# Regrouped blocks of a pair taken from partition quarters of different halves, the second block's transfers issued by ScalarE

## The chip, the cores and the metric

The kernel runs on one core of one Trainium2 chip. The metric is the device time of one execution in microseconds (us), as the median of several executions. The engines are TensorE (PE in the profile, its weight loads PEld), VectorE (DVE), ScalarE (ACT), GpSimd (POOL) and SyncE (SP). SP only issues DMA transfers here; ACT and POOL issue some as well, between their own instructions. In the profile "ACTq" and "SPq" are the issuing sides of ACT and SP.

## The reference

Two parts follow each other. The first filters a sequence along its length with a real FFT; the second is an MLP with a SoLU activation and a layer norm.

```python
x: (8, 3136, 256)   filt_r, filt_i: (1569, 256)
X = rfft(x, axis=1);  y = irfft(X * (filt_r + 1j * filt_i), n=3136, axis=1)

x = y.reshape(25088, 256)            # 25088 tokens
h = x @ w_in                         # (25088, 1024)
e = exp(h - max(h));  sm = e / (sum(e) + 1e-9)
solu = h * sm
ln = (solu - mean(solu)) / sqrt(var(solu) + 1e-6) * g_ln
out = ln @ w_out                     # (25088, 256), float32
```

## The kernel before

**The spectrum part.** Each of the eight sequences goes through a two-stage DFT written as small matmuls, a product with the filter, and the way back. Its results for two sequences at a time lie in the tile `y`. Sequence 0 and part of sequence 1 are done ahead. Then sequence e + 1 is transformed in pieces beside the MLP of sequence e, at steps that the table `PLAN` gives. A "spectrum stage" below is a stretch of steps in which pieces of `Spectrum.forward`, `multiply` and `inverse` run. For each piece ACT issues two loads into SBUF at the end of an even step: `t2` (line L286, 512 KB, called `t<-d` in the profile) and the DFT table `de` (L677, 256 KB). The last spectrum stage ends near 1250 us; from about 1350 us on only the MLP runs, which is called the plain stage.

**The MLP.** Tokens go in blocks of 128, 196 blocks, and two blocks are a pair, 98 pairs. A step `k` belongs to a block; an even and an odd step make a pair `j`. Both matmuls use Strassen's scheme in Winograd's form over a pair: seven products per pair for `w_in` (`product(j, m)`, m from 1 to 7, L717) and seven for `w_out` (`project(p, m)`, L838), with sums of operands by POOL (`sum_of`, L696). Each takes PE about 0.88 us. I call them product m and projection m.

The order of work is written out by hand in `step(k)`, under a manual schedule; each engine takes its instructions in that order.

- Even step of pair j: product 1; projection 5 of pair j-5; product 2; product 6 and its copy to SBUF by ACT (`keep`, L727); projection 3 of pair j-5 and an output half by ACT (`keep_out`, L850); projection 4; the regrouping of the second block of pair j-3; product 7; then, at the end of the step, the loads of the spectrum pieces.
- Odd step: product 5 and its copy to SBUF by ACT (`keep`); projection 1 of pair j-4 with an output half; projection 2; an exponential by ACT (`exponential`, L749); product 3; product 4; projections 6 and 7; the rest.

Product 5 adds to the PSUM bank of product 6, and product 3 adds to that of product 5, so a copy by ACT stands between each two. VectorE's `finish` steps (L738, L741) complete `h` and its running minimum.

**Turning and regrouping.** For the second matmul the block (tokens by features) has to be transposed. VectorE transposes 32 by 32 squares (`turn`, L781) of four blocks into one tile `turn` of two pairs (a group g). Its four partition quarters then hold 32 feature rows each of mixed tokens. `regroup(p, i)` makes from one quarter of 32 partitions a block `solu_t` of 128 partitions, in four transfers of 128 KB, each from the same 32 partitions to one quarter of the destination. A pair has two such blocks (i = 0 and 1), eight transfers in all, which SP issues (L793). The first block's four are issued early in the even step, after `turn`; the second block's four after projection 4, which is the last to read the buffer that the second block goes into (`solu_t1`, two buffers). `a` is the quarter that is read. `out_half` picks the matching column of the scales `rss`, and `store_out` the matching rows of the output; both follow from `a`. `deviations` (L804) and `regroup_deviations` (L810) send the scales through DRAM, also by SP.

Of the kernel before, what the change touches and what calls it, by code (L numbers as in the profile page):

```python
# [17 lines left out]
P = 128  # L18
# [76 lines left out]
def kernel(  # L95
# [10 lines left out]
    nc = tc.nc  # L106
# [290 lines left out]
    with ExitStack() as st:  # L397
# [50 lines left out]
        second = Spectrum(1, None, None, None)  # L448
# [103 lines left out]
        for n in range(16):  # L552
            (nc.sync, nc.scalar)[n % 2].dma_start(
                out=t2_0[NH * (n % 4):NH * (n % 4) + NH, n // 4, :], in_=rows_x[n:n + 1])
# [29 lines left out]
        for i0, n, rows in ((0, 4, P), (4, 4, P), (8, NP - 9, P), (NP - 1, 1, NQ)):  # L584
            f, at = filters[i0]
            nc.sync.dma_start(
                out=f_dram[i0:i0 + n].rearrange("i u q k c -> (u q) i (k c)")[0:rows],
                in_=f[0:rows, at:at + n].rearrange("p i k c -> p i (k c)"))
# [85 lines left out]
    def load_de(sp, u):  # L674
# [6 lines left out]
    turns, variances, solu_ts, solu_sums, rs_rows, rss, pos, ots = (  # L681
        {} for _ in range(8))
# [101 lines left out]
    def regroup(p, i):  # L784


        g, second = divmod(p, 2)
        turned = turns[g].rearrange("p (k q) b i -> p k q (b i)", q=4)
        a = 2 * second + i
        st = upool.tile([P, KF, P], FP32, name=f"solu_t_{p}_{i}", tag=f"solu_t{i}")  # L790
        solu_ts[p, i] = st[:, 0:KF // 2, :], st[:, KF // 2:KF, :]
        for q in range(4):
            nc.sync.dma_start(out=st[32 * q:32 * q + 32, :, :],  # L793
                              in_=turned[32 * a:32 * a + 32, :, q, :])

    def deviations(p):
        g, second = divmod(p, 2)
# [45 lines left out]
    def out_half(p, i, n):  # L843
        if p not in ots:
            ots[p] = wk2.tile([P, 2, C], FP32, name=f"ot_{p}", tag="ot")
        return ots[p][:, i, P * n:P * n + P], rss[p // 2][:, 2 * (p % 2) + i:2 * (p % 2) + i + 1]

    def keep_out(p, i, to):
        rs = out_half(p, i, 0)[1]
        nc.scalar.activation(out=out_half(p, *to)[0], in_=pos[p, 0], func=AFT.Copy, scale=rs)  # L850

    def finish_out(p, i, n, kept, bank):
        ot, rs = out_half(p, i, n)
        nc.vector.scalar_tensor_tensor(out=ot, in0=pos[p, bank], scalar=rs,  # L854
                                       in1=out_half(p, *kept)[0], op0=ALU.mult, op1=ALU.add)

    def store_out(p):
        g, second = divmod(p, 2)

        rows = out[4 * P * g:4 * P * g + 4 * P, :].rearrange("(b a i) c -> a b i c", a=4, i=32)  # L860
        for i in range(2):
            nc.sync.dma_start(out=rows[2 * second + i], in_=ots[p][:, i, :])
        del ots[p]

    blocks = NT * B // 2
# [11 lines left out]
    for e in range(1, B):  # L877
# [5 lines left out]
        for i, t in enumerate(first_at):  # L883
            dma = nc.gpsimd.dma_start
# [17 lines left out]
        for i, t in enumerate(spectrum_at):  # L902
# [5 lines left out]
            dma = nc.sync.dma_start if e == 1 else nc.scalar.dma_start  # L908
# [31 lines left out]
    def step(k):  # L940
# [9 lines left out]
        if not odd:  # L950
# [12 lines left out]
            if 0 <= j - 3 < pairs:  # L963
                regroup(j - 3, 0)
# [15 lines left out]
            if 0 <= j - 3 < pairs:  # L980
                regroup(j - 3, 1)
                deviations(j - 3)
# [8 lines left out]
            if proj:  # L991
                finish_out(p, 1, 0, (1, 0), 1)
                store_out(p)
# [78 lines left out]
```

## Time and profile before

| | us |
|---|---|
| median of 3 runs | 1637.29 |
| lowest, highest | 1636.23, 1648.98 |
| the profiled execution, its own time | 1648.55 |
| its span, first to last instruction | 1646.8 |
| PE busy | 1561.4 (95%) |
| VectorE busy | 1293.3 (79%) |
| GpSimd busy | 1134.6 (69%) |
| ScalarE busy | 902.1 (55%) |

Busy time doesn't count the issuing of DMA transfers. A row of the timeline gives the start and the length in us, the engine, the line, the operation, the tiles as out<-in, the size and the number of instructions that were merged; in square brackets stand the idle time before it and what ended that. A row of waits gives who waited for whom, the total in us, how often, and the longest.

### The profile page before, as it was taken

How to read it: one execution, taken by the hardware profiler on the slowest of the kernel's cores; microseconds unless marked ns; L12 is line 12 of the kernel's file. 1: busy time of each engine (PE TensorE's matmuls, PEld its weight loads, DVE VectorE, ACT ScalarE, POOL GpSimd, SP SyncE). 2: the span in 40 equal slices, each digit the busy share in tenths (PEclk: the TensorE clock that was granted, in tenths of full speed). 3: DMA queues.
4: the chain of work that ended last, by engine and by line, in shares of the span. 5: the costliest groups of instructions: out<-in, count | busy, mean ns of one | idle time of the engine just before them, and what ended most of it. 6: DMA issues, size and time to landing. Idle time of an engine off the chain costs nothing. (4 is left out here: it accounts for less than half of the span.)

```text
span 1646.8 us, 36975 instructions
## 1 busy us (share of the span) xinstructions
PE 1561.4 (95%) x12710; PEld 1055.9 (64%) x12710; DVE 1293.3 (79%) x2633; ACT 902.1 (55%) x1772; POOL 1134.6 (69%) x1325
## 2 busy tenths in 40 slices
PE   5788799999998999999998999999999999999997
PEld 1353366666665676667765676666766777777766
DVE  1686697898888879887887879987898777777772
ACT  2134465566555556566554665656555655666562
POOL 4444686678766875788576967788667665676764
PEclk8999899999999999999999999999999999999999
DMA  9887767876887778876787669766876455444443
GB/s 263 244 272 235 215 195 210 243 216 191 198 239 205 202 190 217 235 200 173 207 230 211 174 164 238 223 189 172 219 206 187 117 130 130 107 107 105 112 109 100
DMA packets 377805, 312.13 MB, mean 190 GB/s; under 512 B 63322, under 2 KB 343395, under 8 KB 377619
## 3 DMA queue, kind: packets, MB, share of 16 engines
q1 hardware_dynamic: 306260, 169.81, 40.4%
q0 software_dynamic: 34464, 101.68, 20.8%
q10 hardware_dynamic: 36896, 38.28, 7.9%
q8 instruction: 103, 1.69, 0.4%
q14 instruction: 82, 0.67, 0.1%
HBM read 124.86 MB, written 81.50 MB: 125 GB/s over the span
## 5 line engine op out<-in xcount | busy, mean ns | idle before, releaser
L838 PEld LDWEIGHTS o<-w_out_sb,solu_t 128*128 128x128 f32 x3136 | 383.6, 193 | 50.3 <-issue 43.0
L717 PE MATMUL m<-w_in_sb,s 128*128 128x512 f32 x784 | 397.7, 609 | 10.7 <-ACT h L727 6.7
L838 PE MATMUL o<-w_out_sb,solu_t 128*128 128x128 f32 x3136 | 402.9, 276 | 4.4 <-DVE ot L854 4.2
L838 PEld LDWEIGHTS o<-w_out_sb,u 128*128 128x128 f32 x2352 | 309.1, 193 | 150.2 <-issue 104.2
L838 PE MATMUL o<-w_out_sb,u 128*128 128x128 f32 x2352 | 313.9, 277 | 11.0 <-ACT ot L850 7.2
L696 POOL TENSOR_TENSOR u<-solu_t 128x512 f32<-128x512 f32 x98 | 134.1, 1368 | 262.8 <-DMA solu_t<-turn 175.4
L717 PE MATMUL m<-w_in_sb,y 128*128 128x512 f32 x588 | 311.1, 613 | 4.2 <-DVE nmax L741 2.3
L727 ACT COPY h<-m 128x512 f32<-128x512 f32 x294 | 173.0, 588 | 251.8 <-PE m L717 211.3
L765 DVE SCALAR_TENSOR_TENSOR h<-e,rsum,h 128x1024 f32<-128x1024 f32 x196 | 288.2, 1471 | 6.9
L850 ACT ACTIVATE ot<-o,rs_t 128x128 f32<-128x128 f32 x392 | 143.7, 367 | 263.1 <-PE o L838 247.8
L741 DVE CUSTOM_DVE_ANT_0 h<-m,h 128x512 f32<-128x512 f32 x196 | 134.2, 684 | 173.4 <-ACT h L727 113.8
L773 ACT ACTIVATE h<-h,nmu 128x1024 f32<-128x1024 f32 x196 | 224.9, 1148 | 44.4 <-DVE turn L781 43.9
L781 DVE STREAM_TRANSPOSE turn<-h 128x1024 f32<-128x1024 f32 x196 | 243.1, 1240 | 3.2
L749 ACT ACTIVATE e<-h,nmax 128x1024 f32<-128x1024 f32 x196 | 225.2, 1149 | 5.8 <-DVE h L765 5.7
L717 PEld LDWEIGHTS m<-w_in_sb,s 128*128 128x128 f32 x784 | 128.9, 192 | 98.6 <-issue 82.6
L696 POOL TENSOR_TENSOR u<-solu_t,u 128x512 f32<-128x512 f32 x98 | 141.7, 1446 | 39.8 <-PE o L838 33.6
L854 DVE SCALAR_TENSOR_TENSOR ot<-o,rs_t,ot 128x128 f32<-128x128 f32 x294 | 102.1, 347 | 82.9 <-ACT ot L850 59.2
L717 PEld LDWEIGHTS m<-w_in_sb,y 128*128 128x128 f32 x588 | 96.9, 193 | 105.4 <-issue 56.7
L696 POOL TENSOR_TENSOR solu_t<-solu_t,solu_t 128x512 f32<-128x512 f32 x98 | 153.8, 1570 | 7.7
L696 POOL TENSOR_TENSOR u<-u,solu_t 128x512 f32<-128x512 f32 x98 | 135.9, 1387 | 0.6
L696 POOL TENSOR_TENSOR s<-y 128x128 f32<-128x128 f32 x196 | 99.9, 510 | 0.5
L367 PEld LDWEIGHTS py<-wb_t,t 50*64 50x64 f32 x3584 | 58.1, 134 | 44.2 <-issue 20.7
(113 smaller groups left out, 1978.2 us busy)
## 6 DMA issues: line engine op xcount, KB each, us to landing
solu_t<-turn SPq DMA_DIRECT2D x784, 128.0 KB
out_dram<-ot SPq DMA_DIRECT2D x196, 128.0 KB
t<-d POOLq DMA_DIRECT2D x112, 200.0 KB, 4.4
d<-x POOLq DMA_DIRECT2D x100, 200.0 KB, 5.3
f<-f_dram POOLq DMA_DIRECT2D x39, 512.0 KB, 8.0
d<-g POOLq DMA_DIRECT2D x39, 512.0 KB, 5.6
t<-d ACTq DMA_DIRECT2D x36, 512.0 KB
x<-in_x_dram SPq DMA_DIRECT2D x112, 98.0 KB
```

The costliest lines, as they stand in the source:

```text
L367: nc.tensor.matmul(out=views[g][64 * h:64 * h + 64, cb, i, :], lhsT=t4[rows, i, c0:c0 + 64], rhs=wb_t[rows, 0:N1], start=True, stop=True)
L696: nc.gpsimd.tensor_tensor(out=out, in0=in0, in1=in1, op=op)
L717: nc.tensor.matmul(out=ms[j, bank], lhsT=lhsT, rhs=w_in_sb[:, w, :], start=m in (1, 2, 7), stop=True, skip_group_check=True)
L727: nc.scalar.copy(out=h_half(k, i), in_=ms[j, 0])
L741: nc.vector.tensor_tensor_reduce(out=h_half(k, i), in0=ms[j, bank], in1=h_half(*kept), scale=1.0, scalar=sofar, op0=ALU.add, op1=ALU.min, ...
L749: nc.scalar.activation(out=e, in_=hs[k], func=AFT.Exp, bias=nmaxs.pop(k)[:, 1:2], scale=-1.0, accum_out=esum)
L765: nc.vector.scalar_tensor_tensor(out=solu, in0=e, scalar=rsum, in1=solu, op0=ALU.mult, op1=ALU.mult, accum_out=nmu)
L773: nc.scalar.activation(out=solu, in_=solu, func=AFT.Square, bias=nmu, scale=-float(DFF), accum_out=variances[g][:, i:i + 1])
L781: nc.vector.transpose(out=turns[g][:, :, i, :], in_=solus[k].rearrange("p (f j) -> p f j", j=32))
L838: nc.tensor.matmul(out=pos[p, bank], lhsT=lhs[:, f, :], rhs=w[:, f, :], start=f == 0 and m in (1, 2, 7), stop=True, skip_group_check=True)
L850: nc.scalar.activation(out=out_half(p, *to)[0], in_=pos[p, 0], func=AFT.Copy, scale=rs)
L854: nc.vector.scalar_tensor_tensor(out=ot, in0=pos[p, bank], scalar=rs, in1=out_half(p, *kept)[0], op0=ALU.mult, op1=ALU.add)
```

## The change

Block i of the pair with the number `second` in its group now reads quarter `second + 2 * i` in place of `2 * second + i`. So a pair's blocks come from quarters 0 and 2, or 1 and 3, where they came from 0 and 1, or 2 and 3: one from the partitions 0 to 63 and one from 64 to 127. The columns of the scales and the rows of the output are picked in the same way. The four transfers of the second block (i = 1) are issued by ACT, at the same place in the program order; the first block's stay with SP.

```diff
 def regroup(p, i):
         g, second = divmod(p, 2)
         turned = turns[g].rearrange("p (k q) b i -> p k q (b i)", q=4)
-        a = 2 * second + i
+        a = second + 2 * i
+        dma = (nc.sync.dma_start, nc.scalar.dma_start)[i]
         st = upool.tile([P, KF, P], FP32, name=f"solu_t_{p}_{i}", tag=f"solu_t{i}")
         solu_ts[p, i] = st[:, 0:KF // 2, :], st[:, KF // 2:KF, :]
         for q in range(4):
-            nc.sync.dma_start(out=st[32 * q:32 * q + 32, :, :],
-                              in_=turned[32 * a:32 * a + 32, :, q, :])
+            dma(out=st[32 * q:32 * q + 32, :, :], in_=turned[32 * a:32 * a + 32, :, q, :])

 def out_half(p, i, n):
-        return ots[p][:, i, P * n:P * n + P], rss[p // 2][:, 2 * (p % 2) + i:2 * (p % 2) + i + 1]
+        return ots[p][:, i, P * n:P * n + P], rss[p // 2][:, p % 2 + 2 * i:p % 2 + 2 * i + 1]

 def store_out(p):
         for i in range(2):
-            nc.sync.dma_start(out=rows[2 * second + i], in_=ots[p][:, i, :])
+            nc.sync.dma_start(out=rows[second + 2 * i], in_=ots[p][:, i, :])
```

The lines after L789 move down by one. In the order of instructions per engine, those of PE, VectorE and GpSimd are the same in both kernels; SP has 98 groups of four transfers fewer and ACT 98 more, each after the output half (L850) of the even step and ahead of the spectrum loads, where there are any, and of the copy of product 5.

## The prediction

> **What bounds the kernel now.** I read the busy table first, then the busy time by stage, then two short stretches of the timeline, and last the answers for the lines that issue transfers.
>
> ```profile
> PE 1561.4 (95%) x12710; PEld 1055.9 (64%) x12710; DVE 1293.3 (79%) x2633; ACT 902.1 (55%) x1772; POOL 1134.6 (69%) x1325
> 902.00:960.00 58.00, 58.00 (x455) 39.87 (x454) 46.48 (x101) 35.99 (x72) 50.40 (x57) 1.00 0.62 171
> 972.00:1074.00 102.00, 101.55 (x975) 69.58 (x973) 92.41 (x178) 58.89 (x118) 71.20 (x83) 1.00 0.80 222
> 1356.00:1594.00 238.00, 238.00 (x1587) 172.84 (x1587) 180.10 (x408) 145.16 (x290) 160.68 (x176) 1.00 0.43 109
> ```
>
> The stage rows give the window, its length, the busy time of PE, PEld, DVE, ACT and POOL, the clock, the DMA share and GB/s. PE has no idle time at all in the plain stages (238.00 of 238.00) and 0.45 us in 102 where spectrum work runs beside the MLP. From 250 to 1600 us TensorE is the bound: what delays a matmul is added in full, and there is little to win. ACT is half idle, but its idle time is in pieces. One pair in the plain stage:
>
> ```profile
> 1494.26 5.36 SPq L793 DMA_DIRECT2D solu_t<-turn  x8
> 1495.79 1.06 PE L838 MATMUL o<-w_out_sb,solu_t 128*128 128x128 f32 x8
> 1496.16 0.37 ACT L850 ACTIVATE ot<-o,rs_t 128x128 f32<-128x128 f32 x1
> 1496.68 1.88 PE L717 MATMUL m<-w_in_sb,s 128*128 128x512 f32 x4
> 1498.60 0.59 ACT L727 COPY h<-m 128x512 f32<-128x512 f32 x1 [2.06 <-PE m L717]
> 1500.18 0.59 PE L717 MATMUL m<-w_in_sb,s 128*128 128x512 f32 x1
> ```
>
> The first PE row is projection 4, the x4 row products 7 and 5, the last row product 3. ACT finishes the output half (L850), is idle for 2.06 us, and copies product 5 out (L727). Product 3 writes the bank that this copy reads, so it can't start before the copy has ended. The transfers take SP 5.36 us for eight, one after the other, while nobody waits for SP.
>
> ```profile
> 972.72 0.38 ACTq L286 DMA_DIRECT2D t<-d  x1
> 973.13 0.52 ACTq L677 DMA_DIRECT2D de<-de_tbl  x1
> 973.44 1.91 SPq L793 DMA_DIRECT2D solu_t<-turn  x3
> 975.17 0.58 ACT L727 COPY h<-m 128x512 f32<-128x512 f32 x1 [2.05 <-PE m L717]
> 429.32 0.37 ACT L850 ACTIVATE ot<-o,rs_t 128x128 f32<-128x128 f32 x1
> 432.60 0.38 ACTq L286 DMA_DIRECT2D t<-d  x1
> 433.02 0.69 ACTq L677 DMA_DIRECT2D de<-de_tbl  x1
> 433.76 0.59 ACT L727 COPY h<-m 128x512 f32<-128x512 f32 x1 [4.07 <-PE o L838]
> ```
>
> In the spectrum stage ACT already issues two loads in this same gap. At 973 they fit in. At 433 they came late, and the copy starts 0.05 us after the second issue has ended: an issue holds ACT's later work back. What an issue costs, in ns (min/median/max):
>
> ```profile
> L793 SPq DMA_DIRECT2D solu_t<-turn x784: 585/626/4077, 167.4 to 1628.1; - x196
> L286 ACTq DMA_DIRECT2D t<-d x42: 338/366/397, 252.4 to 1250.0; - x42
> L677 ACTq DMA_DIRECT2D de<-de_tbl x46: 338/574/2944, 141.1 to 1250.4; - x46
> SPq L793 <- PE o L838: 101.8, 58, 3.8
> ```
>
> The regrouping transfer is a dear one to issue, and its maximum shows that an issue can stall for microseconds. The last row, of SP's waits, is the wait for projection 4 to release the second block's buffer; it goes to ACT with the transfers.
>
> [...] in the plain stage the packets of the eight transfers start about 1.2 us after the first issue and then flow evenly, some 380 in a us, as fast as they are issued. [...]
>
> **The change part by part.**
> *Other quarters.* Both blocks of a pair read the same `turn` tile, which is whole before either is regrouped. Blocks (0,1),(2,3) become (0,2),(1,3); scale column and output rows follow. Same count, sizes and dependences on PE, DVE and POOL: nothing. [...] In the plain stage the first block's issues end as projection 4 releases the second, at 1496.9, so the two still follow each other; I put it at 0, from -3 us (some overlap in the busy stages) to 0.
>
> *SP loses 4 of 8 issues per pair.* SP is not on the path before the end. There, `rows<-rs` (1619.39) stands behind eight issues (1613.61 to 1618.96), and the deviations that the last outputs wait for come after it. Four fewer issues bring it 2.6 us forward: -3.
>
> *ACT gains 98 times four issues, behind the wait for projection 4.* Behind them on ACT are, in order, the two spectrum loads where there are any, the copy of product 5, an output half and an exponential. PE's product 3 waits for the copy. The room: from the end of projection 4 (1496.85, with 0.03 to see it) to product 3 (1500.18), less the copy (0.59) and 0.1: **2.62 us**. This is the figure of nearly all pairs, worked out pair by pair from the trace. The need: SP's undisturbed second block takes 586, 617, 618 and 621 ns with gaps of 0.04: **2.57 us**. Four issues just fit, and nothing else does.
>
> 1. Plain pairs after 1250 us, and pairs between the spectra (about 55): 2.57 into 2.62. Allow 0.05 us each for slips, +3. In the 25 pairs between the spectra SP's second block took 2.9 on average; what is over adds +6.
> 2. Pairs with the two loads: 41 of them. The loads hold ACT for 1.28 us on average, and the room there is 3.06 on average (some pairs have a PE wait already). 2.57 + 1.28 - 3.06 is 0.79; summed pair by pair, with none below nothing, **+37 us**. This is a floor: it takes every regrouping issue at its undisturbed time.
> 3. Stalls of issues in these 41 pairs. SP's second block took 4.15 us there, not 2.57. If ACT's issues stall alike, the pair-by-pair sum is 100 us instead of 37, +63. SP's blocks had its own first four ahead of them and ACT's don't; but SP's first blocks, with a freer queue, were no quicker (sum of four 3.16 us on average against 3.03). I take half, +32. The `t` load, never over 397 ns, now stands behind four transfers; I price it like a `de` load behind a `t` load, 0.2 us more: +8.
>
> So 3 + 6 + 37 + 32 + 8 = 86. Against it: PE's idle time between 250 and 1250 us, about 12 us, of which half may absorb delays (-6), the end (-3), and blocks that land sooner because SP is free (-2). **Net +75 us.** DVE's idle time before the copy (1.98 us a pair) takes its shift of 0.7 us. The profiled execution (1648.55, span 1646.8) would go to 1724; it is 11 us above the median of the runs, 1637.29, which goes to **1712**.
>
> **The rivals.**
> *A: issues on ACT stall little (only the floor).* 37 + 3 + 6 less 11, +35 at most, with more absorbed +20: 1657 to 1672. For it: in the plain stage issues hardly ever stall. Against: DMA share 0.8 in the spectrum stage.
> *B: it stalls more.* All of SP's excess, a stalled `t`[...]: 100 + 9 + 20 + 10, about +140: 1777. ACT waits for a completion semaphore that eight transfers of both queues use in turn, so it can also wait for SP's older transfers. For it: issues of 2 to 4 us exist.
> *C: faster.* The place is the gap of 2.06 us on ACT. If ACT issued this transfer as it issues `t` (0.37 us), four take 1.6 us, and with the loads 2.9, within the 3.06: no cost. Then SP's relief counts: half of PE's 20 us of idle time between 300 and 1350 us and 5 at the end, -15: 1622. It decides below 0.4 us an issue. For it: `t` is four times as large and cheaper; against it: of the 512 KB `t` loads, SP issued some early on, in 388 ns (median) where ACT takes 366, so the shape sets the price, not the engine.
> *D: no change that can be told*: the floor is absorbed by PE's waits and the gains. 1637 to 1653.
>
> **How the numbers follow.** Forecast (+40 to +125) 0.60; A 0.17; B 0.08; D 0.10; C 0.05. About 1% is what can be told from no change. A reaches below 1653.7 hardly at all. Faster 0.05, same 0.10, slower 0.85. The range 1655 to 1775 takes in the forecast, A and half of B, and leaves out C, D and the worst of B.
>
> **What would show it.** On ACT, four `solu_t` rows of about 0.6 us directly after L850, waiting for PE o L838; L727 waiting less for PE m; PE idle before product 3, "PE m L717 <- ACT h L727" growing from 6.7 us to tens; pair periods of 12.26 us unchanged after 1356, and longer in 430 to 500, 597 to 700 and so on. If the plain period grows by 0.3 us or more, the issue is dearer on ACT than on SP; if the spectrum stages don't grow, step 2 is wrong.

## The result and the profile after

The change makes the kernel a third slower: 2168.74 us (median, 2157.77 to 2171.24) against 1639.21 us for the kernel before on the same chip, a ratio of 1.320 with a 95% interval of 1.313 to 1.328. The forecast was 1712 with a range up to 1775. The direction was right, the size was not: +530 us where +75 was forecast.

The profiled execution has a span of 2168.7 us. From its page: the busy table, the clock that TensorE was granted (in tenths, over 40 slices), the chain of waits by engine, and the group of ScalarE's copies L727, three in a pair, product 5's among them (busy time and mean ns, then the idle time before them and what ended most of it). The second block has the clock and the same group of the kernel before.

```profile
PE 1692.3 (78%) x12710; PEld 1123.9 (52%) x12710; DVE 1272.8 (59%) x2633; ACT 895.6 (41%) x1772; POOL 1121.9 (52%) x1325
PEclk9998888898878988889988898888988899999999
...
PE 40%; DMA 26%; DVE 8%; ACT 7%; issue 6%; POOL 6%; ACTq 4%; SPq 3%; DVEq 0%; POOLq 0%
...
L727 ACT COPY h<-m 128x512 f32<-128x512 f32 x294 | 172.8, 588 | 733.0 <-DMA solu_t<-turn 375.0
```

```profile
PEclk8999899999999999999999999999999999999999
...
L727 ACT COPY h<-m 128x512 f32<-128x512 f32 x294 | 173.0, 588 | 251.8 <-PE m L717 211.3
```

TensorE was the bound with 95% and is now busy for 78%. Its idle time went from 85 to 476 us (span less busy time), +391. The other +131 us are busy time: the same 12710 matmuls take 1692.3 us in place of 1561.4, at a mean granted clock of 0.892 where it was 0.981 (how this goes with the gaps stands in the part on the clock). A quarter of the chain of waits is now transfers. ACT stands idle for 733 us before the copies L727, half of it behind the new transfers; before the change it was 252 us, most of it a wait for the product that is to be copied.

The answers for waits of the changed kernel (waiting row, releaser: total us, times, longest us) show the path from there to TensorE. The last row is the first one's counterpart in the kernel before:

```profile
PE m L717 <- ACT h L727: 391.8, 80, 10.5
DVE h L741 <- ACT h L727: 617.1, 96, 12.6
...
ACT h L727 <- DMA solu_t<-turn: 375.0, 48, 14.8
ACT h L727 <- DMA rs_t<-rows: 118.1, 10, 13.8
ACT h L727 <- DMA x<-in_x_dram: 70.1, 7, 11.9
ACT h L727 <- DMA out_dram<-ot: 18.3, 2, 9.9
...
PE m L717 <- ACT h L727: 6.7, 4, 4.3
```

L717 is the line of all seven products of `w_in`, but in the changed kernel the waits are product 3's: in the trace product 5 waits 0.1 us in all. Product 3 waits for the copy 391.8 us, which is 385 more than before and so nearly all of TensorE's new idle time. And the copy waits for transfers with which it has nothing to do: `rs_t`, `x` and `out` are issued by SyncE, and no operand of L727 comes from them. This is the line to stop at.

By stage (length; busy PE, PEld, DVE, ACT, POOL; clock, DMA share, GB/s), two windows with spectrum work and one plain one, and last a window with spectrum work of the kernel before:

```profile
300.00:450.00 150.00, 106.49 (x968) 71.77 (x967) 83.99 (x166) 53.46 (x109) 67.78 (x83) 0.84 0.52 144
1350.00:1500.00 150.00, 103.15 (x852) 68.42 (x850) 79.58 (x160) 53.72 (x109) 65.03 (x80) 0.83 0.49 142
1950.00:2100.00 150.00, 142.18 (x791) 100.84 (x790) 105.51 (x234) 82.53 (x166) 104.42 (x106) 1.00 0.42 102
...
300.00:450.00 150.00, 147.19 (x1338) 100.33 (x1330) 130.64 (x258) 87.71 (x174) 116.51 (x134) 1.00 0.78 207
```

TensorE idles for 30% of the spectrum stages at a clock of 0.84, and for only 5% of the plain stage. Against the kernel before all engines fall together, DMA too (share 0.52 where it was 0.78): nothing is saturated, everybody waits in turn.

One bad pair, from the timeline:

```profile
1020.42 0.37 ACT L850 ACTIVATE ot<-o,rs_t 128x128 f32<-128x128 f32 x1
1020.92 1.88 PE L717 MATMUL m<-w_in_sb,s 128*128 128x512 f32 x4
1021.12 7.84 ACTq L794 DMA_DIRECT2D solu_t<-turn  x4
1021.33 0.34 SPq L804 DMA_DIRECT2D rows<-rs  x1
1021.77 1.30 SPq L862 DMA_DIRECT2D out_dram<-ot  x2
1023.17 3.28 SPq L810 DMA_DIRECT2D rs_t<-rows  x4
1026.56 3.57 SPq L794 DMA_DIRECT2D solu_t<-turn  x4
1029.00 0.59 ACT L727 COPY h<-m 128x512 f32<-128x512 f32 x1 [8.21 <-DMA solu_t<-turn]
1029.73 2.04 PE L717 MATMUL m<-w_in_sb,s 128*128 128x512 f32 x2 [5.14 <-ACT h L727]
```

Four transfers take ACT 7.84 us, not 2.57. The single records show where: they start at 1021.12, 1021.77, 1022.81 and **1028.37**, and each of these takes about 0.6 us. The fourth waited 4.95 us for something. In the trace each transfer of SyncE or ScalarE names the semaphore that gets the signs of its landing. There are eight of these for both queues (108 to 112, 114, 115 and 117), each named by 203 or 204 of the 1627 transfers, and the two queues merge into one order in which every transfer takes the next of the eight. 1586 of the 1627 wait, in the issue or just before it, for the semaphore that they name themselves, which the transfer eight places earlier in that order names too. Here the order is: ACT's first, `rows`, two output stores, ACT's second, two `rs_t`, ACT's third, two `rs_t`, the first transfer of the next pair's first block on SyncE, ACT's fourth. Eight before ACT's fourth is the second output store. SyncE issued that from 1022.48 to 1023.08, *after* ACT had begun its block. The last of that store's five signs comes at 1028.35, 5.3 us after the end of its issue, and ACT's fourth issue starts 0.02 us later. The copy starts at 1029.00, 0.04 us after that issue has ended: it, and with it DVE and product 3, waited for an output store.

Counted in this order over the whole program, 95 of ScalarE's transfers and filter loads wait for a transfer that SyncE was given later than the first of ScalarE's block: 37 output stores, 32 x loads, 17 `rs_t`, and a few others. In the trace ACT stands idle for some 250 us just before these 95. In 66 of them it is idle for more than 0.3 us, and each of the 66 starts within 0.06 us of the last sign on the semaphore that it waits for. (Of ScalarE's 245 transfers with no idle time before them, only 3 start so close to one.) Before all its other regrouping transfers and filter loads, nearly 400, it is idle for 131 us; 41 of these are before the first of a block, which also waits for projection 4, and of the 52 other waits of more than 0.3 us, 51 end in the same way with the landing of an *earlier* transfer.

### The profile page after: what moved, and what is told of

It is laid out like the page before. It is cut to its first block, busy times and chain, and to the rows that moved or that the text cites. A ratio compares the mean times of both kernels' runs of the same rounds, so it can differ in the third digit from the quotient of the medians.

```text
span 2168.7 us, 36785 instructions
## 1 busy us (share of the span) xinstructions
PE 1692.3 (78%) x12710; PEld 1123.9 (52%) x12710; DVE 1272.8 (59%) x2633; ACT 895.6 (41%) x1772; POOL 1121.9 (52%) x1325
## 4 chain that ended last, share of the span: by engine, by line
PE 40%; DMA 26%; DVE 8%; ACT 7%; issue 6%; POOL 6%; ACTq 4%; SPq 3%; DVEq 0%; POOLq 0%
PE m L717 17%; PE o L838 13%; DMA solu_t<-turn 9%; DMA x<-in_x_dram 6%; DMA out_dram<-ot 4%; ACTq L794 3%; ACT h L727 3%; DMA rs_t<-rows 3%; PE pc L296 2%; ACT e L749 2%; PE pa L264 2%; POOL u L696 2%; PE py L367 2%; DVE h L765 1%; DVE turn L781 1%
## 5 line engine op out<-in xcount | busy, mean ns | idle before, releaser
L717 PE MATMUL m<-w_in_sb,s 128*128 128x512 f32 x784 | 449.4, 677 | 412.8 <-ACT h L727 391.8
L727 ACT COPY h<-m 128x512 f32<-128x512 f32 x294 | 172.8, 588 | 733.0 <-DMA solu_t<-turn 375.0
L838 PEld LDWEIGHTS o<-w_out_sb,u 128*128 128x128 f32 x2352 | 343.3, 211 | 179.2 <-issue 134.0
L838 PEld LDWEIGHTS o<-w_out_sb,solu_t 128*128 128x128 f32 x3136 | 391.1, 196 | 44.1 <-issue 43.0
L717 PEld LDWEIGHTS m<-w_in_sb,s 128*128 128x128 f32 x784 | 137.3, 205 | 514.9 <-issue 453.5
L717 PE MATMUL m<-w_in_sb,y 128*128 128x512 f32 x588 | 354.2, 690 | 3.0 <-DVE h L738 1.5
L838 PE MATMUL o<-w_out_sb,u 128*128 128x128 f32 x2352 | 342.3, 293 | 12.7 <-ACT ot L850 12.7
L765 DVE SCALAR_TENSOR_TENSOR h<-e,rsum,h 128x1024 f32<-128x1024 f32 x196 | 280.9, 1433 | 6.9
L850 ACT ACTIVATE ot<-o,rs_t 128x128 f32<-128x128 f32 x392 | 144.1, 368 | 311.2 <-PE o L838 297.8
L717 PEld LDWEIGHTS m<-w_in_sb,y 128*128 128x128 f32 x588 | 112.0, 217 | 127.5 <-issue 48.7
L338 POOL DMA_DIRECT2D d<-g x46 | 35.4, 769 | 208.2 <-ACT g L334 192.9
L696 POOL TENSOR_TENSOR s<-y 128x128 f32<-128x128 f32 x196 | 90.8, 463 | 0.5
```

The lines of the kernel that those rows point to most:

```text
L696: nc.gpsimd.tensor_tensor(out=out, in0=in0, in1=in1, op=op)
L717: nc.tensor.matmul(out=ms[j, bank], lhsT=lhsT, rhs=w_in_sb[:, w, :], start=m in (1, 2, 7), stop=True, skip_group_check=True)
L727: nc.scalar.copy(out=h_half(k, i), in_=ms[j, 0])
L765: nc.vector.scalar_tensor_tensor(out=solu, in0=e, scalar=rsum, in1=solu, op0=ALU.mult, op1=ALU.mult, accum_out=nmu)
L838: nc.tensor.matmul(out=pos[p, bank], lhsT=lhs[:, f, :], rhs=w[:, f, :], start=f == 0 and m in (1, 2, 7), stop=True, skip_group_check=True)
```

## Experiments

All medians are of runs beside the kernel before on the same chip (1639 to 1642 us). "Theory S" is the shared semaphores; the rivals are named in the expectations.

| kernel | median us | ratio to before (95%) |
|---|---|---|
| new quarters, all on SyncE | 1646.0 | 1.002 (0.998 to 1.005) |
| old quarters, second block on ScalarE | 2178.4 | 1.329 (1.325 to 1.334) |
| before + 7 small copies on ScalarE | 1652.2 | 1.009 (1.006 to 1.012) |
| before + 9 small copies on ScalarE | 1685.4 | 1.028 (1.023 to 1.033) |
| ScalarE issues 3 of the 4 | 1954.7 | 1.191 (1.187 to 1.195) |
| ScalarE issues 2 of the 4 | 1678.9 | 1.023 (1.017 to 1.029) |
| ScalarE issues the first block, SyncE the second | 1731.7 | 1.056 (1.049 to 1.062) |
| after, no output stores, no scales by DRAM | 1822.3 | 1.113 (1.105 to 1.120) |
| before, with the same left out | 1632.8 | 0.996 (0.994 to 0.998) |
| after, output stores to 128 rows in one piece | 1989.9 | 1.214 (1.208 to 1.220) |
| before, with the same destination | 1627.9 | 0.992 (0.990 to 0.994) |

### Which part of the change

```diff
-        dma = (nc.sync.dma_start, nc.scalar.dma_start)[i]
+        dma = nc.sync.dma_start
```

> The new choice of quarters alone, all eight transfers of a pair issued by SyncE as before. Theory S (ScalarE's in-order queue waits for completion semaphores that it shares with SyncE's later transfers): the quarters have no part in the 530 us, so 1639 within 8 us. Rival Q (the quarters make the transfers land later[...], so the cost is theirs): well above 1700.

Measured: 1646.0 us, no difference that can be told. The other half alone, the kernel before with ScalarE's queue:

```diff
         a = 2 * second + i
+        dma = (nc.sync.dma_start, nc.scalar.dma_start)[i]
...
-            nc.sync.dma_start(out=st[32 * q:32 * q + 32, :, :],
-                              in_=turned[32 * a:32 * a + 32, :, q, :])
+            dma(out=st[32 * q:32 * q + 32, :, :], in_=turned[32 * a:32 * a + 32, :, q, :])
```

> The issuing engine alone: the old quarters, the second block of each pair issued by ScalarE. Theory S: all of the loss is here, as the order in which the transfers take the completion semaphores is that of the changed kernel: 2169 within 25 us. Rival Q: well below 2169; if the two parts need each other, somewhere between.

Measured: 2178.4 us. The whole loss is in the engine that issues, the quarters neither help nor hurt.

### ScalarE's time, without any transfer

```diff
                 regroup(j - 3, 1)
+                if proj:
+                    fill = small.tile([P, P], FP32, name=f"fill_{j}", tag="fill", bufs=1)
+                    nc.scalar.copy(out=fill, in_=pos[p, 1])
+                    for _ in range(6):
+                        nc.scalar.copy(out=fill, in_=fill)
```

> The kernel before, all transfers by SyncE, with seven small copies added on ScalarE at the place where the changed kernel issues its four transfers: the first reads projection 4's bank, so it waits for projection 4, the others copy a scratch tile onto itself, in all about 2.5 us by an estimate from the 0.37 us of the 128x128 output half. They take ScalarE's time as the four issues were to do in the prediction, and no completion semaphore. Theory S: as the prediction's steps 1 and 2 have it, +20 to +90 us, so 1660 to 1730. Rival I (the time of four issues in that gap is enough to lose 530 us, by pushing the copy, DVE and TensorE's clock in a chain): above 1950.

Measured: 1.009, that is +15 us, a little below what theory S gave and far from rival I. As seven copies are less than four issues, the full dose was run too, with `range(8)`:

> As the run with small copies on ScalarE, with nine of them in place of seven. The seven took 0.27 + 6 x 0.30 = 2.05 us, less than the 2.57 of four undisturbed issues; nine take 0.27 + 8 x 0.30 = 2.65 us. It gives the price of ScalarE's time alone at the full dose. Steps 1 and 2 of the prediction said +46 in all for it: 1670 to 1700. If the small loss of the run with seven came only from its smaller dose, and the gap is a cliff: above 1800.

Measured: 1.028, +46 us. From the page of this run and its answers for waits:

```profile
PE 1564.5 (93%) x12710; PEld 1052.7 (63%) x12710; DVE 1275.9 (76%) x2633; ACT 1144.3 (68%) x2636; POOL 1119.6 (66%) x1325
PEclk8999999999999999999999999999999999999999
PE m L717 <- ACT h L727: 31.7, 30, 1.8
```

ACT is made *busier* by 242 us, and product 3 waits for the copy 31.7 us in all and 1.8 us at the longest. There is no cliff in this gap. TensorE's busy time (1564.5 us against 1561.4) and its mean clock (0.990 against 0.981) hardly move. So the time of four issues is worth 46 us, and some 480 us of the loss come from what transfers do and copies don't.

### Fewer transfers on ScalarE

```diff
-            dma(out=st[32 * q:32 * q + 32, :, :], in_=turned[32 * a:32 * a + 32, :, q, :])
+            dma = nc.scalar.dma_start if i and q in (0, 1, 2) else nc.sync.dma_start
+            dma(out=st[32 * q:32 * q + 32, :, :], in_=turned[32 * a:32 * a + 32, :, q, :])
```

> The changed kernel, but ScalarE issues three of the second block's four transfers and SyncE the last one. In the program built, the fourth transfer was the one whose semaphore belonged to a later transfer of SyncE: with three, no regrouping transfer on ScalarE waits for a transfer of SyncE that was emitted after the block's first, but the filter loads behind them still do (the second of each pair of loads for an output store 32 times, the first for a regrouping transfer of SyncE 21 times). Theory S: the pairs with an output store in the way and no loads lose nothing, those with loads still wait: 1700 to 1900, less than half of the 530. Rival I: three quarters of the time issued, so about three quarters of the loss, 2000 to 2050.

Measured: 1954.7 us, outside what theory S gave (1700 to 1900) and below rival I. The pairs tell more than the total. Product 3 is called late here by the time between the end of projection 4 and its own start that goes beyond 3.33 us, the figure of an undisturbed pair. In the 50 pairs without filter loads, whose regrouping transfers wait for none of SyncE's later ones, it comes 0.36 us late on average (the changed kernel: 2.31). In the pairs with loads where there is such a wait (34), it comes 6.5 us late. These 34 make 221 us, more than two thirds of this kernel's loss of 312. The waits moved from the transfers to the loads behind them, which the answers for waits show:

```profile
PE m L717 <- ACT h L727: 238.6, 56, 9.6
...
ACT h L727 <- DMA t<-d: 114.2, 12, 12.1
ACT h L727 <- DMA solu_t<-turn: 108.4, 20, 9.3
```

The theory had the right pairs, but I had under-priced the waits of the loads.

> The changed kernel, but ScalarE issues two of the second block's four transfers and SyncE the other two. 8 waits of ScalarE for a later transfer of SyncE (6 for regrouping transfers, 2 for x loads, all on the second filter load); issue time on ScalarE 1.25 us a pair, which with the loads' 1.28 stays within the 3.06 of room. Theory S: 8 waits of up to 7 us and a few us of stalls: 1645 to 1700. Rival P: half of the transfers, about half of the loss: 1850 to 1950.

The same edit with `(0, 1)`. Measured: 1678.9 us, within theory S. Half of the transfers cost 7% of the loss.

### As many transfers, other semaphores

```diff
-        dma = (nc.sync.dma_start, nc.scalar.dma_start)[i]
+        dma = (nc.scalar.dma_start, nc.sync.dma_start)[i]
```

> The changed kernel with the two queues exchanged: ScalarE issues the first block of each pair, SyncE the second. As many transfers on ScalarE, of the same size, at the same price, and all the work is done. In the order in which the program gives out the eight semaphores, only 4 of ScalarE's transfers then wait for a later one of SyncE, for 95 in the changed kernel. Theory S: most of the loss goes: 1645 to 1730. Rival P (392 regrouping transfers on ScalarE are the cost, wherever they stand): at least half of it stays, above 1900.

Measured: 1731.7 us, at the upper edge of theory S and far from rival P. The same number of the same transfers on ScalarE costs 92 us here and 530 in the changed kernel. The first block stands elsewhere in ScalarE's order, so this run alone doesn't separate place from semaphores. What it loses, it loses at another product: the copy of product 6 now stands behind the four issues, and product 5 waits for it (product 3 waits 3 us in all).

```profile
PE m L717 <- ACT h L727: 62.5, 52, 5.0
```

The next kernel leaves ScalarE's queue as it is in the changed kernel and takes away most of what it waits for:

```diff
-            rs_rows[g] = rows = rs_dram.tile([P, 4], FP32, name=f"rows_{g}", tag="rows")
-            nc.sync.dma_start(out=rows, in_=rs)
+            rs_rows[g] = rs
...
-        for i in range(2):
+        for i in range(2 if p >= 96 else 0):
             nc.sync.dma_start(out=rows[second + 2 * i], in_=ots[p][:, i, :])
```

(`regroup_deviations` then hands `rs` on, without its four transfers, and `rs` has four buffers in place of two.) Most output rows stay unwritten and the scales are those of other rows, so this kernel can only measure.

> The changed kernel without two kinds of SyncE's transfers: the output stores (but for the last two pairs, so most output rows stay unwritten) and the scales' way through DRAM (rows and rs_t; the scale tile is used as it is, so the rows get scales of other rows). ScalarE's four transfers and two filter loads stay as they are. In the program built, the waits on ScalarE for a transfer that SyncE was given after the block's first fall from 95 to 13. Theory S: 13 waits of about 8 us at most, plus the issue time as in the small-copies run (+15) and what the stalls add (about +30): 1680 to 1790. Rival P (ScalarE's transfers are slow for their own sake: stalls from the packets in flight, or the landing of its own four): most of the loss stays, above 1950.

> The kernel before with the same two kinds of transfers left out (most output rows unwritten, scales of other rows): what leaving them out is worth by itself. All theories: TensorE is the bound, so 1635 to 1645, apart from a few us at the end, where the way through DRAM was on the path: 1625 to 1645.

Measured: 1822.3 us, and 1632.8 for the same omissions without the change. So the change costs 189 us where it cost 530: about 340 us come with the output stores and scale transfers, while leaving them out is worth 6 us by itself. The omission takes away their traffic too, and it shifts the rotation: of the 32 waits for a later x load, 12 are left. The runs with three and with two transfers on ScalarE, which move as many bytes as the changed kernel, speak for the waits and not the traffic. A kernel that does nothing but give ScalarE's transfers semaphores of their own was not run. But 1822 is above the 1790 that I allowed. The page and the waits of this run:

```profile
PE 1615.0 (89%) x12710; PEld 1082.1 (60%) x12710; DVE 1274.8 (70%) x2633; ACT 894.2 (49%) x1772; POOL 1111.5 (61%) x1325
PE m L717 <- ACT h L727: 122.4, 49, 7.7
```

TensorE's busy time is still 54 us above that of the kernel before: waits of up to 7.7 us are left, and I had put nothing for the clock. The idle time in front of ScalarE's transfers that is due to SyncE's later ones fell to 16 us; that of all others is 129 us, as good as unchanged. 40 us of this is before the first transfer of a block, which also waits for projection 4. Before the others ScalarE is idle for more than 0.3 us 49 times, and 47 of these end within 0.06 us of a landing on the semaphore waited for: that of an x load given *shortly before* the block (some 40 us), of one of ScalarE's own transfers (22 us) or of SyncE's regrouping (20 us). So in this run, too, most of the waits are for the rotation.

### How long the awaited stores take to land

```diff
-        rows = out[4 * P * g:4 * P * g + 4 * P, :].rearrange("(b a i) c -> a b i c", a=4, i=32)
+        rows = out[4 * P * g:4 * P * g + 4 * P, :].rearrange("(a p) c -> a p c", a=4)
```

> The changed kernel with another destination of the output stores: 128 rows in one piece per block in place of four groups of 32 (the rows stand in another order in the output). The same transfers in the same order on the same semaphores[...]. 37 of the 95 waits of ScalarE for a later transfer of SyncE are for an output store, which takes about 6 us from issue to landing in the traces read. Theory S with a landing time set by the destination's shape: the stores land in 2 to 3 us, 37 waits lose some 3 to 4 us each, with the clock's share 120 to 180 us: 1990 to 2050. If the landing time comes from the traffic and not from the shape: 2169 within 25 us.

> The kernel before with the same other destination of the output stores (rows in another order). Nobody waits long for SyncE there: 1639 within 8 us by every theory.

Measured: 1989.9 us, 179 less than the changed kernel, as theory S with a landing time set by the shape had it, and at the edge of its numbers; the kernel before gains 0.8% by the same edit, or 13 us, which is more than I allowed. (The rows stand in another order in the output, so these two kernels only measure as well.) Every semaphore and its order are as before. What changes is the landing: from the end of the issue to the last sign it is 4.40 us for a store in the changed kernel and 2.67 here (medians). Other transfers land sooner as well, an x load after 4.45 us in place of 5.39, so not all of the gain comes from waits for stores.

The traces show what the shape does. With four groups of 32 rows every store that can be followed (191 of 196) gives its semaphore five signs, and the stores' packets of 1 KB run most often four at a time (between 1905 and 1935 us, at most seven); with 128 rows in one piece there are sixteen signs, and up to 21 packets run at once (1750 to 1790 us).

Over the 37 waits for an output store, the time from the end of the store's issue to the start of ScalarE's next transfer was 5.90 us on average in the changed kernel, and 36 of the 37 stood idle for it by more than 0.3 us. Here it is 3.58 us for the 29 that still do, and the idle time before the 37 falls from 155 to 63 us. The plain stage changes too. First two successive pairs of the changed kernel there, then two of this one, from the timelines:

```profile
1909.63 3.80 ACTq L794 DMA_DIRECT2D solu_t<-turn  x4
1914.20 1.10 PE L717 MATMUL m<-w_in_sb,s 128*128 128x512 f32 x2 [1.15 <-ACT h L727]
...
1923.27 2.65 ACTq L794 DMA_DIRECT2D solu_t<-turn  x4
1926.69 1.10 PE L717 MATMUL m<-w_in_sb,s 128*128 128x512 f32 x2
```

```profile
1753.65 2.63 ACTq L794 DMA_DIRECT2D solu_t<-turn  x4
1756.33 0.59 ACT L727 COPY h<-m 128x512 f32<-128x512 f32 x1 [3.05 <-PE o L838]
...
1766.54 2.65 ACTq L794 DMA_DIRECT2D solu_t<-turn  x4
1769.23 0.59 ACT L727 COPY h<-m 128x512 f32<-128x512 f32 x1 [2.85 <-PE o L838]
```

In the changed kernel every other pair's issues stall, here to 3.80 us, and product 3 waits. With the other destination the four issues of the plain stage sum to 2.57 us a pair on average, where the changed kernel has 3.05. (SyncE's second block in the kernel before sums to 2.44; the prediction's 2.57 has the gaps between the issues in it, and with gaps ScalarE's median here is 2.64.) So the stores' destination was worth 0.48 us a pair in these issues as well.

No version tried that computes and stores the same beats the kernel before. The nearest with transfers on ScalarE is the one with two, at +2.3%.

## Why the prediction was wrong, by its steps

*What bounds the kernel.* Right, and it is why the loss is so large: TensorE, busy for 95%, had no slack to absorb delays.

*Other quarters: 0.* Right (1.002).

*Four fewer issues on SyncE bring the end 3 us forward.* Not measured by itself; beside +530 it can't be seen.

*The issue is as dear on ScalarE as on SyncE.* Right within some 5% (2.57 us against 2.44 for four undisturbed ones), as the answers for the line show too (min/median/max in ns). That disposes of rival C, which needed 0.4 us or less. What the price of an issue leaves out is the rotation: the two queues share eight semaphores, and 95 of ScalarE's transfers and filter loads wait for a later one of SyncE's.

```profile
L794 SPq DMA_DIRECT2D solu_t<-turn x392: 585/650/3065, 166.2 to 2143.9; - x196
L794 ACTq DMA_DIRECT2D solu_t<-turn x392: 592/622/2559, 173.5 to 2148.9; - x196
```

*Steps 1 and 2, room against need: 3 + 6 + 37 = 46 us.* Right, and not by luck: nine small copies in the same gap measured +46 by the ratio, and they fall where the steps put them. Against the kernel before, product 3 is later by 38 us in the pairs with loads, by 5 in those between the spectra and by 6 in the plain ones (forecast: 37, 6 and 3). The method, room less need pair by pair, holds for work that only takes time. The statement that plain pairs cost 0.05 us each does not hold for the transfers: product 3 was 0.91 us late there, because of the stalls of every other pair.

*Step 3, stalls: +40.* **This is the step that failed.** It took the stalls that SyncE's issues had in the kernel before (4.15 us a block in place of 2.57) as the measure for ScalarE's, and took half. But what held ScalarE up was not the transfer's own stall: it was the wait for the eighth-last transfer that the rotation names. In the kernel before, 114 of the 1627 transfers in the rotation are ScalarE's, and for 1398 of SyncE's 1513 the one eight places earlier is SyncE's own, issued before in the same order. In the changed kernel 506 are ScalarE's, and for 384 of these the eighth-last is SyncE's. In the 95 it was one that SyncE was given only after ScalarE's block had begun, and where it was an output store, ScalarE's next transfer started 5.90 us after the end of the store's issue on average. And step 3 confined the cost to the 41 pairs with loads: 18 pairs without loads had such a wait too, 4.1 us late each, 74 us in all. The 35 pairs with loads and a wait came 8.33 us late each, 291 us. These 53 pairs make 365 of the 434 us by which product 3 came late between the pairs 5 and 97.

*Rival B, 1777.* It named the right thing, a completion semaphore that transfers of both queues use in turn (in the traces of both kernels there are eight, each taken by every eighth transfer), and then looked the wrong way: "SP's older transfers". Those left ScalarE idle for 88 us; the later ones for 250. It had a chance of 0.08, and the last 10 us of its sum were an allowance for the clock.

*The clock.* The sum of the forecast had no term for it. TensorE's busy time rose by 131 us. The changed kernel's trace records two levels of the granted clock, full and half: 472.5 us in all at half, in 65 stretches, where the kernel before has 65.8 us in 12. From the start of one matmul of L717 to that of the next it is 431 ns at the full clock and 854 at half (medians). After the first 250 us TensorE has 39 idle gaps of 5 us or more, and with each a stretch at half the clock begins, inside the gap or within 1 us of its end. With the 24 gaps between 2 and 5 us this is so for 13, and with the 36 between 0.2 and 2 us for none. The busy time follows the longest wait of product 3: with at most 1.8 us, in the run of nine copies, the term is 3 us; with 7.7 us, in the run without stores and scales, it is 54; with 10.5 us it is 131.

So the loss of 530 us can be set out by differences between runs: 46 for ScalarE's time; about 143 more when real transfers take that time, with output stores and scale transfers absent (189 less 46; waits for x loads and regrouping blocks, longer issues and a lower clock, 0.954 on average, are all seen in that trace); and about 340 when these are there again. How the 143 divide between landings, issues and the clock was not separated, and neither were the stores' places in the rotation from their traffic in the 340.

*Range and chances.* Faster 0.05, same 0.10 and slower 0.85 were right in direction; the range ended at 1775, because the rival that reached beyond was bounded by waits for transfers that had already been issued.

*What would show it.* "PE m L717 <- ACT h L727" was to grow from 6.7 us to tens and grew to 391.8. The plain period was to stay: over the last 19 it is 12.5 us on average before and 13.7 after. The test "if the plain period grows by 0.3 us or more, the issue is dearer on ACT" would have misled: it grew, and the undisturbed issue costs nearly the same. The stage that was to grow, the one with spectrum work, did.

## What to carry to other kernels

Before a transfer is moved to another engine, write down for each what it waits for, its completion semaphore included, in the order in which the program hands these out. Here the queue was that of a computing engine: its wait for another engine's later transfer held the copy behind it back, and the price was the landing time of that transfer (5.90 us after the end of its issue on average for an output store) and not the 0.6 us of the issue. A gap of 2.62 us that just fits four issues had no room for such a wait.

Replacing a transfer by compute of the same length in the same place is a cheap way to tell the price of time from the price of waiting: here 46 us against 530.

## What the runs showed that I had not expected

- How long a store of 128 KB kept its semaphore went with the destination's shape: 4.40 us after the issue (median) with four groups of 32 rows, its packets most often four at a time, and 2.67 with 128 rows in one piece (the same bytes). ScalarE's issues went with it too: 3.05 us for four in the plain stage with the first shape, against 2.57.
- Engine time and queue time are not alike: 242 us of additional compute on ScalarE cost 46 us; 392 issues of about the same length cost 530.
- A third of TensorE's waiting came back as slower matmuls: 391 us more idle, and 131 us more busy at a mean clock of 0.892 (0.981 before).
